# The last tokens' product with v, in three parts between the groups of h

## The chip, the cores and the metric

The kernel runs on one core of a Trainium2 chip. A core has five engines that run side by side, each with its own instruction stream: TensorE (PE, the matmuls; its weight loads are listed apart as PEld), VectorE (DVE), ScalarE (ACT), GpSimd (POOL) and SyncE (SP, which here issues nearly all transfers). Data lies in SBUF, results of matmuls in PSUM; a transfer (DMA) moves data between HBM and SBUF or within SBUF. The metric is the time of one execution on the device in microseconds (us); lower is better.

## The reference

Eight batches of eight heads, each with 576 tokens of 64 numbers, all in float32. Attention with a threshold: per row only the scores within tau of the row's maximum count. The result, 4,608 tokens of 512 numbers, goes through a feed-forward block.

```python
scores = scale * np.matmul(q, k.transpose(0, 1, 3, 2))
thresh = np.max(scores, axis=-1, keepdims=True) - tau
scores = np.where(scores >= thresh, scores, -1000000000.0)
attn = np.exp(scores - np.max(scores, axis=-1, keepdims=True))
attn = attn / (np.sum(attn, axis=-1, keepdims=True) + 1e-09)
x = np.matmul(attn, v)            # then (B,H,S,D) -> (B*S, H*D)
h = x @ w_in                      # 4608 x 512 @ 512 x 1024
solu = h * softmax(h)
ln = (solu - mean(solu)) / np.sqrt(var(solu) + 1e-06) * g_ln
out = ln @ w_out                  # 4608 x 1024 @ 1024 x 512
```

## The kernel before

**Tiles.** Two heads are always worked on at once. A batch's 576 tokens are 512 (two kinds, 0 and 1, of 256 tokens) and the last 64 (kind 2). The work of attention is a list of 144 slots, 18 for each batch: 8 for kind 0 and 8 for kind 1 (four pairs of heads, two slots each), and 2 for kind 2, in which two pairs of heads share a slot. A slot is 128 rows of scores for each of two heads.

**TensorE.** Nearly all matmuls are done on quarters of the array, 64 x 64, four side by side. A float32 matmul of the program appears in the trace as two weight loads and two matmuls, so four instructions; a group of four matmul records is one in each quarter.

**Rounds.** The main loop (lines 784 to 924) does one round for each slot and writes out the order of every engine by hand; nothing is reordered afterwards. In a round, TensorE gets first the transposes that fit beside the scores, then the scores of the slot (L412: 8 matmuls), then one step of the feed-forward block and, if one is due, one product with v. The steps of the feed-forward block for a tile of 128 tokens are: h in two halves of 512 columns (L572, `ff_h`, 16 matmuls each, in two successive rounds), and o in two halves (L676, `ff_o`, 32 matmuls each, later). The product with v (L516, `attend_steps`) multiplies v by the transposed attention `wT`; for kinds 0 and 1 it has 36 matmuls with 128 columns, and for kind 2 it has 72 with 64 columns, one such product for each batch. `attend_steps` is a generator: each step of it issues one matmul.

**The other engines in a round.** DVE takes the maxima of the scores (L434), ACT forms the ramp and the exponentials (L449, L458), POOL normalises (L468), DVE transposes (L480), and SP moves the result into `wT` in four transfers (L491); the product follows at least two rounds later. For h, DVE takes the maximum (L587), ACT the exponential (L596), DVE multiplies (L602), and so on until ACT or DVE writes the normalised tile V (L638, L643), which is transposed for o (L664). The output tile is copied out of PSUM by ACT (L691).

**PSUM.** Two tiles, s0 and s1, hold the scores. Two more, p0 and p1, are handed out in turn by `take` to h, to the products and to o. h keeps its tile until DVE has multiplied (L602); a product's is free after ACT has copied it into `xh` or `xe` (L539); that of o after ACT's copy into `ob` (L691). In a round that starts h and also has a product, h takes one tile and the product the other.

**Around the change.** When a product of kind 2 is due in a round that also has a half of h, the round passes the generator to `ff_h` as `beside`. The 16 matmuls of a half of h go in four groups of four (`c` from 0 to 3); after a group, `ff_h` may take a number of steps from the generator. Any rest is issued after `ff_h` by the round itself (lines 896 to 898). After the product comes ACT's copy into `xe` (`attended`, L539). In the first half of h a small instruction on POOL (`fence`, L107) waits for its last four matmuls, and the second half waits for that. For h tiles made after the last slot, `ff_h` uses the whole array (L562) and does nothing with `beside`.

Of the eight products of kind 2, seven are placed beside h: those of the batches 0, 2, 4 and 6 beside a second half, and those of 1, 3 and 5 beside a first half. The eighth comes after the last slot.

## Time and profile before

| what | value |
|---|---|
| median of five runs | 900.38 us (897.79 to 903.31) |
| the profiled execution | 897.58 us |
| its span, first to last instruction | 895.6 us |
| PE busy | 848.5 us, 95% |
| DVE busy | 680.6 us, 76% |
| ACT busy | 591.0 us, 66% |
| POOL busy | 452.7 us, 51% |
| L572, one matmul of h, 512 columns | 589 ns, 1856 records |
| L516, one matmul of a product, 64 or 128 columns | 264 ns on average, 5760 records |

The profile is of one execution, whose own time is the span and some 2 us around it. Matmuls overlap each other: a record's length says how long one took to pass through, not how far apart two can start. In a row of the timeline the first number is the start in us from the span's start, the second the length of the merged row, and the bracket at the end the idle time of the engine before it with what ended it. "issue" there means that the engine waited for nothing that the profile shows.

### The profile page before, as it was taken

How to read it: one execution, taken by the hardware profiler on the slowest of the kernel's cores; microseconds unless marked ns; L12 is line 12 of the kernel's file. 1: busy time of each engine (PE TensorE's matmuls, PEld its weight loads, DVE VectorE, ACT ScalarE, POOL GpSimd, SP SyncE). 2: the span in 40 equal slices, each digit the busy share in tenths (PEclk: the TensorE clock that was granted, in tenths of full speed). 3: DMA queues.
4: the chain of work that ended last, by engine and by line, in shares of the span. 5: the costliest groups of instructions: out<-in, count | busy, mean ns of one | idle time of the engine just before them, and what ended most of it. 6: DMA issues, size and time to landing. Idle time of an engine off the chain costs nothing. (4 is left out here: it accounts for less than half of the span.)

```text
span 895.6 us, 39683 instructions
## 1 busy us (share of the span) xinstructions
PE 848.5 (95%) x17089; PEld 646.1 (72%) x17089; DVE 680.6 (76%) x1312; ACT 591.0 (66%) x1241; POOL 452.7 (51%) x871
## 2 busy tenths in 40 slices
PE   5667899999999999999999999999999999999997
PEld 3445578877687777887787777878778787777655
DVE  5999786888777768777777777777877877887451
ACT  5866676777677767777677776677767776676121
POOL 2555555555555555555655555555555555555120
PEclk9688899999999999999999999999999999999999
DMA  7999989796867776876887777777877766766322
GB/s 241 257 240 243 216 191 206 180 214 159 202 158 176 164 177 158 189 175 159 188 187 179 164 160 185 182 175 157 190 184 176 179 134 146 167 139 134 78 48 48
DMA packets 95502, 154.61 MB, mean 173 GB/s; under 512 B 27224, under 2 KB 69216, under 8 KB 95328
## 3 DMA queue, kind: packets, MB, share of 16 engines
q1 hardware_dynamic: 94192, 150.09, 72.1%
q8 instruction: 134, 2.20, 1.1%
q10 hardware_dynamic: 1136, 2.00, 0.7%
q14 instruction: 40, 0.33, 0.1%
HBM read 46.14 MB, written 9.44 MB: 62 GB/s over the span
## 5 line engine op out<-in xcount | busy, mean ns | idle before, releaser
L434 DVE CUSTOM_DVE_ANT_0 w<-s_ps,tau_t 128x576 f32<-128x576 f32 x280 | 200.8, 754 | 135.0 <-PE s_ps L412 114.5
L449 ACT ACTIVATE w<-s_ps,nth 128x576 f32<-128x576 f32 x280 | 202.0, 744 | 120.0 <-DVE nth L434 97.4
L676 PE MATMUL o_ps<-w,uT 64*64 64x256 f32 x4608 | 269.3, 376 | 2.0 <-DVE uT L664 1.0
L676 PEld LDWEIGHTS o_ps<-w,uT 64*64 64x64 f32 x4608 | 232.1, 133 | 46.2 <-issue 11.9
L468 POOL TENSOR_SCALAR w<-w,sm 128x576 f32<-128x576 f32 x288 | 218.7, 772 | 14.3
L572 PE MATMUL h_ps<-w,xh 64*64 64x512 f32 x1856 | 220.9, 589 | 1.9 <-issue 1.9
L458 ACT ACTIVATE w<-w,ntau 128x576 f32<-128x576 f32 x288 | 220.4, 772 | 0.0
L480 DVE STREAM_TRANSPOSE T<-w 128x576 f32<-128x576 f32 x288 | 206.0, 751 | 5.6 <-POOL w L468 5.1
L516 PEld LDWEIGHTS pv<-wT,v 64*64 64x64 f32 x5760 | 170.1, 136 | 38.1 <-issue 23.1
L412 PE MATMUL s_ps<-kT,qT 64*64 64x64 f32 (+1 forms) x2048 | 175.4, 426 | 13.8 <-ACT w L449 12.8
L516 PE MATMUL pv<-wT,v 64*64 64x128 f32 (+1 forms) x5760 | 172.3, 264 | 7.4 <-DMA wT<-T 3.8
L572 PEld LDWEIGHTS h_ps<-w,xh 64*64 64x64 f32 x1856 | 114.1, 133 | 86.4 <-issue 62.7
L465 POOL TENSOR_SCALAR sm<-sm 128x2 f32<-128x2 f32 x144 | 37.5, 261 | 260.7 <-ACT w L458 257.8
L466 POOL TENSOR_TENSOR sm<-sm,mone 128x2 f32<-128x2 f32 x144 | 105.1, 730 | 12.0
L412 PEld LDWEIGHTS s_ps<-kT,qT 64*64 64x64 f32 x2048 | 68.6, 140 | 22.3 <-ACT w L449 18.1
L638 ACT ACTIVATE V<-u,nb,rs 128x1024 f32<-128x1024 f32 x36 | 44.7, 1241 | 52.7 <-POOL nb L628 52.7
L539 ACT COPY xh<-pv 128x256 f32<-128x256 f32 x64 | 23.7, 371 | 65.5 <-PE pv L516 65.5
L587 DVE TENSOR_REDUCE hm<-h_ps 128x1 f32<-128x1024 f32 x36 | 43.1, 1198 | 19.3 <-PE h_ps L572 13.1
L458 ACT ACTIVATION_READ_ACCUMULATOR w<-w,ntau 128x1 f32 x288 | 57.0, 198 | 0.0
L596 ACT ACTIVATE u<-h_ps,hm 128x1024 f32<-128x1024 f32 x36 | 40.3, 1119 | 19.2 <-DVE hm L587 13.9
L664 DVE STREAM_TRANSPOSE uT<-V 128x1024 f32<-128x1024 f32 x36 | 43.9, 1220 | 9.0 <-DMA V<-u 8.9
L602 DVE TENSOR_TENSOR u<-h_ps,u 128x1024 f32<-128x1024 f32 x36 | 42.8, 1189 | 10.0 <-ACT u L596 10.0
(81 smaller groups left out, 632.6 us busy)
## 6 DMA issues: line engine op xcount, KB each, us to landing
wT<-T SPq DMA_DIRECT2D x288, 288.0 KB, 5.8
V<-u SPq DMA_DIRECT2D x144, 64.0 KB, 3.7
out_dram<-ob SPq DMA_DIRECT2D x71, 128.0 KB, 3.0
v<-in_v_dram SPq DMA_DIRECT2D x16, 512.0 KB, 6.8
v<-in_v_dram SPq DMA_DIRECT2D x32, 256.0 KB, 5.7
q<-in_q_dram SPq DMA_DIRECT2D x15, 512.0 KB, 6.5
k<-in_k_dram SPq DMA_DIRECT2D x15, 512.0 KB, 6.4
raw<-in_moe_w_out_dram SPq DMA_DIRECT2D x8, 512.0 KB, 7.6
```

The costliest lines, as they stand in the source:

```text
L412: nc.tensor.matmul(out=ps[h][ROWS[y], ks], lhsT=lhsT, rhs=d["kT"][ROWS[h], ks], start=True, stop=True,)
L434: nc.vector.tensor_tensor_reduce(out=w, in0=ps[:, 0:S], in1=(zero if loose else tau_t).to_broadcast([P, S]), scale=1.0, scalar=BIG, op0=AL ...
L449: nc.scalar.activation(out=d["w"][x], in_=d["w"][x] if d["loose"] else d["ps"][x][:, 0:S], func=AF.Prelu, bias=d["nth"][x], scale=-1.0, al ...
L458: nc.scalar.activation(out=w, in_=w, func=AF.Exp, bias=ntau, scale=1.0, accum_out=sm[:, x : x + 1])
L466: nc.gpsimd.tensor_tensor(out=sm, in0=sm, in1=mone, op=ALU.pow)
L468: nc.gpsimd.tensor_scalar(out=w, in0=w, scalar1=sm[:, x : x + 1], scalar2=1.0, op0=ALU.mult, op1=ALU.mult)
L480: nc.vector.transpose(out=T[:, :, r, h, :], in_=w)
L516: nc.tensor.matmul(out=to, lhsT=d["v"][ROWS[u], h0 + h, m ^ 4 * u if m < 8 else m], rhs=rhs, start=m == 0, stop=m == NK - 1,)
L572: mm = nc.tensor.matmul(out=h[ROWS[y], f], lhsT=x[ROWS[r], c, ROWS[y]], rhs=w1_parts[ROWS[r], c, part ^ r], start=part == 0 and c == 0, st ...
L638: nc.scalar.activation(out=V, in_=u, func=AF.Identity, bias=nb, scale=rs)
L664: nc.vector.transpose(out=uT, in_=d["V"].rearrange("p y (m x) -> p m y x", x=32))
L676: nc.tensor.matmul(out=d["o"][ROWS[z], 512 * r : 512 * r + 256], lhsT=d["uT"][ROWS[r], m].rearrange("p y x -> p (y x)"), rhs=w2[ROWS[r], m ...
```

## The change

Before, the 72 matmuls of a product of kind 2 are issued after the third group of h (in the code also after the fourth, but then none are left). After, 24 are issued after the second, the third and the fourth group each.

```diff
                     if part and not last:
                         sync(mm, d["fence"])
                     last.append(mm)
-            for _, _ in zip(range(72 * (c > 1)), beside):
+            for _, _ in zip(range(24 * (c > 0)), beside):
                 pass
         if part == 0:
             d["fence"] = fence(last[-4:])
```

So TensorE's order, in matmuls of the program, goes at seven places from 12 of h, 72 of the product, 4 of h to 8 of h, 24 of the product, 4 of h, 24 of the product, 4 of h, 24 of the product. The order on DVE, ACT, POOL and SP stays, and so do all instructions and the waits that they carry.

## The prediction

> **What bounds the kernel now.** I read the page's head and busy rows first, then the clock row, then the list of waits, and then TensorE's own order of time around the seven places that the diff touches.

> ```profile
> span 895.6 us, 39683 instructions
> PE 848.5 (95%) x17089; PEld 646.1 (72%) x17089; DVE 680.6 (76%) x1312; ACT 591.0 (66%) x1241; POOL 452.7 (51%) x871
> PE   5667899999999999999999999999999999999997
> PEclk9688899999999999999999999999999999999999
> q8 instruction: 134, 2.20, 1.1%
> ```

> TensorE is busy in 95% of the span and in nine tenths or more of every slice from about 130 us on, at full clock. No other engine comes near. Busy is no proof of a bound, since a matmul's recorded length (589 ns for 512 columns) overlaps the next one; so I looked at the starts. Groups of four matmuls start 0.43 us apart in h with no hole, and between 100 and 880 us there are only eleven holes of more than 0.6 us between the starts of two TensorE records. So a microsecond more or less on TensorE's queue in this stretch is a microsecond in the span, and what happens on DVE, ACT or POOL counts only if TensorE then waits.

> Eight of those eleven holes have one thing in common. If all TensorE records (weight loads, matmuls, semaphore instructions) are numbered in order of start, each of the eight stands before a number that leaves 193 when divided by 256: at 104, 139, 226, 236, 332, 538, 648 and 743 us. The queue of kind "instruction" in the fence moves 2.20 MB in 134 packets, 16,384 bytes each: 256 instructions of 64 bytes. These are waits for the engine's own instructions, and three of the eight lie inside the product that the change moves. The third place, in TensorE's order of time:

> ```profile
> 330.28 1.90 PE L516 MATMUL pv<-wT,v 64*64 64x64 f32 x114
> 333.82 0.38 PE L516 MATMUL pv<-wT,v 64*64 64x64 f32 x9 [1.64 <-issue]
> 333.99 0.61 PE L572 MATMUL h_ps<-w,xh 64*64 64x512 f32 x3
> ...
> 334.10 1.02 PE L572 MATMUL h_ps<-w,xh 64*64 64x512 f32 x5
> 334.85 1.25 PE L412 MATMUL s_ps<-kT,qT 64*64 64x64 f32 x16
> ```

> The product has nine tenths of its matmuls done, then TensorE stands still for 1.64 us although it waits for no engine and no transfer ("issue"), and goes on. At 538 us the same hole is 0.43 us and at 743 us 0.70 us. In starts the three cost more: h and the product take 5.54 us where nothing stalls (below), here 7.45, 6.20 and 6.57 us from h's start to the next scores, so 1.91, 0.66 and 1.03 us. The instruction packet that ends the hole at 333.8 us ran from 331.19 to 332.25 us, 1.57 us before work resumed; at the other two the distance is 1.25 and 1.49 us.

> At the fourth and sixth place the product starts late for another reason, seen in the row of weight loads and in ACT's:

> ```profile
> 437.01 0.24 PEld L572 LDWEIGHTS h_ps<-w,xh 64*64 64x64 f32 x4 [0.19 <-issue]
> 437.83 1.30 PEld L516 LDWEIGHTS pv<-wT,v 64*64 64x64 f32 x78 [0.58 <-ACT ob L691]
> ```
> ```profile
> 436.07 1.24 ACT L638 ACTIVATE V<-u,nb,rs 128x1024 f32<-128x1024 f32 x1 [1.20 <-POOL nb L628]
> 437.21 0.57 ACT L691 COPY ob<-o_ps 128x512 f32<-128x512 f32 x1
> ```

> The product's PSUM pair is given back by the copy of an output tile on ACT, which ends at 437.78 us. Today that costs nothing: the last group of h before the product starts at 437.55 us and the product at 437.87 us, exactly in step. But there is no reserve.

> [...] the product's first weight loads run 0.32 us before its first matmul, under h. So a seam between h and the product need not cost anything.

> **The change part by part.** It removes and adds nothing: no instruction, no wait, no transfer; DVE, ACT, POOL and SP keep their order. Since the count is the same, the 256-instruction boundaries fall on the same numbers. Only TensorE's order changes, at seven places (the eighth batch's product goes beside h that isn't split, and stays).

> Prices, from the first place, where nothing stalls: the product's 72 matmuls (144 records) take from 134.38 to 136.48, 2.10 us, so 24 take 0.70 us; four matmuls of h (8 records, the starts 136.48 to 137.34) take 0.86 us. The order 12 h, 72, 4 h becomes 8 h, 24, 4 h, 24, 4 h, 24. Sum either way 16 x 0.215 + 2.10 = 5.54 us. Hence the product starts 0.86 us earlier and ends 0.86 us later, and h ends 0.70 us earlier.

> *Seams.* There are three more changes between the two kinds at each place. From h into the product the step is 0.32 to 0.43 us, h's own; from the product into h the first h matmul starts 0.01 us after the last of the product. I take zero; with a seam at 0.05 us (a few product matmuls' spacing of 15 ns) it would be 21 x 0.05 = 1.05 us lost, and a gain has no ground.

> *Instruction stalls in the product (third, fifth, seventh place).* Count instructions from h's start, four per matmul. One boundary is crossed at about number 55, the next at 311. Before, 55 lies 7 into the product and 311 lies 263 into it: both in the dense stretch, 256 x 7.3 ns = 1.9 us apart. After, 55 lies 23 into the first third and 311 lies 55 into the last: 1.72 + 0.17 = 1.89 us and 1.72 + 0.70 + 0.86 + 0.70 + 0.86 + 0.40 = 5.24 us from h's start, 3.35 us apart. At the third place h starts at 327.40 and instructions resume at 333.81, 6.4 us later. If the fetch lands when it does now, 1.2 us of stall stays, but only 41 instructions (0.30 us) stand behind it and no h: the window ends at 334.1 rather than 334.85, 0.74 us gained. If the fetch follows the crossing, which comes 0.74 us earlier, 1.4 us is gained. At 538 us instructions resume 5.16 us from h's start, before they are wanted: all 0.66 us gained. At 743 us they resume 5.54 us from it, 0.3 us late: 0.73 us gained, or all 1.03. Together 2.1 us, between 1.3 (fetches that come 0.4 us later each) and 3.1.

> *Stalls just after the window.* The hole at 139 us (0.97 us) belongs to the fetch of a boundary at number 152, in the product's first half before, in the second third after, crossed at the same time (3.34 us from h's start)[...] I take 0.4. The one at 648 us (a step of 0.91 us between starts where 0.32 is usual: 0.59 us) is absorbed by the delay of the sixth place, below.

> *Lost cover, fourth and sixth place.* The product now wants its pair at 437.01 and gets it at 437.83; the wait is no longer under h. 0.82 us each, 1.64 us, less the 0.59 us at 648: 1.05 us lost. Behind the waiting weight load stand the other eight matmuls of h and the next scores; those feed DVE, ACT and POOL, all with less load.

> *Lost cover, wT.* At the third and fifth place the last piece of wT is issued at 322.84 and 528.70 us and lands 6.3 us later, 329.1 and 535.0 us. The product's first matmul comes at 329.98 and 535.85 now, and would at 329.12 and 534.99: reserve 0.86 before, none after. In this profile it costs 0.0; a transfer that is later by some tenths costs them. I take 0.2 us for both, between 0 and 1.7.

> *The end of the product.* ACT's copy of xe starts 0.86 us later relative to the window. At the odd places the next o takes that pair: the copy (0.37 us) ends about 0.64 us after the product, o's weights then load in 0.13 us, and o's first matmul comes 0.97 us after the scores start. Hidden by the scores; 0. ACT is idle there (its idle before the copy is up to 2.5 us); if it ran an exponential of 0.77 us at that moment, up to 0.5 us would be lost.

> *h earlier.* The maximum on DVE starts 0.7 us earlier at the odd places, and the next scores' maximum some 0.3 us. TensorE's next scores start at 339.28, 0.4 us after their release by ACT at 338.88, so it doesn't wait for these now: 0 gained.

> Sum: -2.1 - 0.4 + 1.05 + 0.2 = -1.25 us, a span of 894.4; with the bounds above, -1.3 to -3.8 of gains and 1.05 to 3.8 of losses. The profiled execution took 897.6 us with a span of 895.6, 2.8 us below the median of 900.38. Taken off the median: 899.1 us.

> **Rivals.** (1) *The stalls were longer in the other runs.* The profiled run is the fast end; if the three in the product are each about 2 us elsewhere, 1.4 us is won at each, 4.2 + 0.4 - 1.25 = 3.35 us, 897.0. For it: instruction packets start anywhere from 2.2 us before to 4.2 us after the crossing of their boundary in this trace. Against: only three boundaries. (2) *Slower: the start of the product becomes a wait.* ACT's copy at 437.2 and 642 us, and wT at three places, come after TensorE wants them. From 0 reserve each further 0.1 us late costs 0.1; all 0.86 us at five places would be 4.3 us, against a gain of 2.5: 902.2. It decides as soon as the five waits average over 0.5 us. For it: two of them are at 0.82 in the trace. Against: the other three stand at 0 or have 0.3 us over (743 us). (3) *Nothing moves*: fetches and the copy shift along with TensorE; 900.4.

> **How the numbers follow.** Forecast 0.50, rival 1 0.17, rival 2 0.15, rival 3 0.18. The five runs spread by 5.5 us, so a median is good to about 1.2 us, and about 0.5% (4.5 us) is what can be told from no change. No case in its middle reaches that: 0.08 faster, from the tail of rival 1; 0.05 slower, from that of rival 2; 0.87 same. The range, from rival 1 with some scatter to most of rival 2, is 896.0 to 902.2.

> **What would show it.** Right: in TensorE's order of time the holes "issue" inside the product at about 333, 538 and 743 us are gone or below 1.2 us; at about 437 and 642 us the product's first weight load waits some 0.8 us for the copy of ob; the starts of h and of scores elsewhere keep their 0.43 us. Wrong: waits for wT of over 0.3 us at several places, or new holes at other 256-instruction boundaries, or a step of more than 0.5 us at a seam.

## The result and the profile after

| | before | after |
|---|---|---|
| median of the comparison | 898.42 us (893.13 to 904.42, 71 runs) | 896.87 us (892.65 to 900.46, 36 runs) |
| ratio | 1 | 0.9976, 95% interval 0.9965 to 0.9987 |
| span of the profiled execution | 895.6 us | 895.6 us |

By the ratio the change wins 0.24%, some 2.2 us; forecast were 1.25 us and "no change that counts". On two more occasions, told below, the ratio was 1.0004 and 0.9988, with intervals that include 1. So the gain is between nothing and a quarter of a per cent. Ratios leave out runs that lie more than 1.5% above the fastest of their kernel.

The page of the changed kernel, its head, busy row and TensorE's slices:

```profile
span 895.6 us, 39683 instructions
PE 849.3 (95%) x17089; PEld 663.1 (74%) x17089; DVE 681.0 (76%) x1312; ACT 591.4 (66%) x1241; POOL 452.5 (51%) x871
PE   5667899999999999999999999999999999999997
```

Nothing has moved at this height: the same bound, the same instructions, and by chance the same span. In the profile after, the first h that the change touches starts at 133.00 us rather than 131.81, so 1.2 us had been lost before the change could act. The difference has to be looked for at the seven places (numbered in order of time, one for each of the batches 0 to 6). At the third, TensorE's row of time now reads:

```profile
330.43 0.91 PE L516 MATMUL pv<-wT,v 64*64 64x64 f32 x43
...
331.30 1.03 PE L572 MATMUL h_ps<-w,xh 64*64 64x512 f32 x6
331.99 1.33 PE L516 MATMUL pv<-wT,v 64*64 64x64 f32 x47
333.11 0.23 PE L412 MATMUL s_ps<-kT,qT 64*64 64x64 f32 x3
```

The hole of 1.64 us is gone; the last third of the product takes 1.33 us, 0.42 us longer than the third before it (0.91 us). At the fifth place it went the other way:

```profile
536.98 0.67 PE L516 MATMUL pv<-wT,v 64*64 64x64 f32 x29
539.10 0.50 PE L516 MATMUL pv<-wT,v 64*64 64x64 f32 x18 [1.45 <-issue]
539.39 0.23 PE L412 MATMUL s_ps<-kT,qT 64*64 64x64 f32 x3
```

Here 1.45 us of "issue" where the kernel before had 0.43, at the same boundary of a 256-instruction block. And at the fourth place the lost cover, in the weight loads' row and in ACT's:

```profile
434.42 0.24 PEld L572 LDWEIGHTS h_ps<-w,xh 64*64 64x64 f32 x4 [0.19 <-issue]
436.09 0.83 PEld L516 LDWEIGHTS pv<-wT,v 64*64 64x64 f32 x46 [1.43 <-ACT ob L691]
```
```profile
434.33 1.24 ACT L638 ACTIVATE V<-u,nb,rs 128x1024 f32<-128x1024 f32 x1 [1.19 <-POOL nb L628]
435.47 0.57 ACT L691 COPY ob<-o_ps 128x512 f32<-128x512 f32 x1
```

ACT's copy ends at 436.04 us as late in the round as before, and the product that is now wanted 0.86 us sooner waits for it. In the list of waits the second of these rows is one that the kernel before doesn't have; the first was 2.8 us there, in three waits:

```profile
PE pv L516 <- issue: 2.5, 3, 1.4
PE pv L516 <- ACT ob L691: 1.0, 2, 0.5
```

Three profiles of the changed kernel and two of the one before were taken in all. The length of each place, from the first matmul of h to the first matmul of something else, in us (5.53 where nothing stalls):

| kernel | 1 | 2 | 3 | 4 | 5 | 6 | 7 | sum |
|---|---|---|---|---|---|---|---|---|
| before | 5.53 | 5.53 | 7.45 | 5.56 | 6.19 | 5.56 | 6.56 | 42.4 |
| before, again | 5.53 | 5.53 | 10.11 | 5.54 | 6.44 | 5.54 | 6.52 | 45.2 |
| after | 5.53 | 6.00 | 5.95 | 6.41 | 7.34 | 6.41 | 6.20 | 43.8 |
| after, again | 5.53 | 5.64 | 5.95 | 6.41 | 6.30 | 6.41 | 5.88 | 42.1 |
| after, third | 5.53 | 5.99 | 5.91 | 6.39 | 5.59 | 6.39 | 6.31 | 42.1 |

Places 2, 4 and 6 are longer by 0.1 to 0.9 us every time, 1.8 to 2.2 us together. Places 3, 5 and 7 are shorter on the whole and vary. What lies outside the places counts too. Summing all steps between TensorE's starts that stand at a block boundary (record number leaving 193 on division by 256), from 100 to 870 us, where the step is over 0.45 us, less 0.25 us each: 7.7 and 10.0 us before, 2.9, 5.3 and 4.2 us after. I call this the sum of block waits below.

That sum can be tested against the time. From the start of h at place 1 to the end of the span, the 14 profiles of this document took 758.5 to 771.2 us. Three things are taken off: the block waits of that stretch, the waits of the product's first weight load at places 2, 4 and 6 (counted in the same way), and half of any stretch at half clock (1.7 us each, in four profiles; see the last section). Twelve profiles are then left with 756.8 to 758.1 us. The other two, 759.7 and 759.9 us, are the two versions below that put idle matmuls in front of the kernel before; their 2 us are not explained. In the first pair of profiles the block waits of that stretch fall from 6.6 to 2.9 us, and the waits of the product's weights rise from nothing to 2.2 us.

### The profile page after: what moved, and what is told of

It reads as the page before. It is cut to its first block, busy times and chain, and to the rows that moved or that the text cites. A ratio compares the mean times of both kernels' runs of the same rounds, so it can differ in the third digit from the quotient of the medians.

```text
span 895.6 us, 39683 instructions
## 1 busy us (share of the span) xinstructions
PE 849.3 (95%) x17089; PEld 663.1 (74%) x17089; DVE 681.0 (76%) x1312; ACT 591.4 (66%) x1241; POOL 452.5 (51%) x871
## 2 busy tenths in 40 slices
PE   5667899999999999999999999999999999999997
## 5 line engine op out<-in xcount | busy, mean ns | idle before, releaser
L676 PEld LDWEIGHTS o_ps<-w,uT 64*64 64x64 f32 x4608 | 235.9, 133 | 41.8 <-ACT xh L539 10.1
L572 PE MATMUL h_ps<-w,xh 64*64 64x512 f32 x1856 | 223.7, 590 | 0.2 <-issue 0.2
L516 PEld LDWEIGHTS pv<-wT,v 64*64 64x64 f32 x5760 | 176.5, 136 | 43.9 <-issue 21.6
L412 PE MATMUL s_ps<-kT,qT 64*64 64x64 f32 (+1 forms) x2048 | 177.8, 426 | 13.9 <-ACT w L449 12.9
L516 PE MATMUL pv<-wT,v 64*64 64x128 f32 (+1 forms) x5760 | 177.1, 264 | 8.6 <-DMA wT<-T 4.1
L572 PEld LDWEIGHTS h_ps<-w,xh 64*64 64x64 f32 x1856 | 122.2, 134 | 72.4 <-issue 40.2
L412 PEld LDWEIGHTS s_ps<-kT,qT 64*64 64x64 f32 x2048 | 69.7, 141 | 20.3 <-ACT w L449 18.5
L638 ACT ACTIVATE V<-u,nb,rs 128x1024 f32<-128x1024 f32 x36 | 44.7, 1241 | 52.9 <-POOL nb L628 52.9
L602 DVE TENSOR_TENSOR u<-h_ps,u 128x1024 f32<-128x1024 f32 x36 | 42.8, 1189 | 10.8 <-ACT u L596 10.8
L664 DVE STREAM_TRANSPOSE uT<-V 128x1024 f32<-128x1024 f32 x36 | 43.8, 1218 | 6.8 <-DMA V<-u 6.8
```

What stands on the lines that cost most here:

```text
L412: nc.tensor.matmul(out=ps[h][ROWS[y], ks], lhsT=lhsT, rhs=d["kT"][ROWS[h], ks], start=True, stop=True,)
L516: nc.tensor.matmul(out=to, lhsT=d["v"][ROWS[u], h0 + h, m ^ 4 * u if m < 8 else m], rhs=rhs, start=m == 0, stop=m == NK - 1,)
L572: mm = nc.tensor.matmul(out=h[ROWS[y], f], lhsT=x[ROWS[r], c, ROWS[y]], rhs=w1_parts[ROWS[r], c, part ^ r], start=part == 0 and c == 0, st ...
L638: nc.scalar.activation(out=V, in_=u, func=AF.Identity, bias=nb, scale=rs)
L664: nc.vector.transpose(out=uT, in_=d["V"].rearrange("p y (m x) -> p m y x", x=32))
L676: nc.tensor.matmul(out=d["o"][ROWS[z], 512 * r : 512 * r + 256], lhsT=d["uT"][ROWS[r], m].rearrange("p y x -> p (y x)"), rhs=w2[ROWS[r], m ...
```

## The experiments

Two questions: is the hole "issue" a wait for the engine's instructions, and how do the gain and the lost cover split? Theory A is that of the prediction. B: the gain comes from the order on TensorE as such, or from h ending earlier. C: the holes belong to something else at those places.

### The two kinds of place apart

Three parts only where the product stands beside a second half of h (places 1, 3, 5, 7):

```diff
-            for _, _ in zip(range(72 * (c > 1)), beside):
+            for _, _ in zip(range(24 * (c > 0) if part else 72 * (c > 1)), beside):
```

> Three parts of 24 only where the product stands beside a second half of h (places 1, 3, 5, 7); beside a first half (2, 4, 6) the 72 stay behind the third group. Theory A (spreading the product shortens the waits for instruction blocks, and starting it earlier costs cover at places 4 and 6, and at 2 as the profile after shows): keeps the gain, loses none of the cover, so 1 to 2 us faster than the changed kernel, 3 to 4 us (0.35 to 0.45%) faster than the kernel before, and no weight load of the product waits for the copy of ob. Theory B (the gain comes alike from all seven places, from the order on TensorE alone): four sevenths of the changed kernel's 2.15 us, 1.2 us.

Measured: 895.23 us against 899.02 us, ratio 0.9961 (0.9941 to 0.9981). Places 2, 4 and 6 are back at 5.53 to 5.54 us, 3, 5 and 7 at 6.09, 5.53 and 6.28; the sum of block waits is 1.4 us. At the fourth place the weight load waits for the copy again only under h:

```profile
434.52 0.31 PEld L572 LDWEIGHTS h_ps<-w,xh 64*64 64x64 f32 x4
435.33 1.79 PEld L516 LDWEIGHTS pv<-wT,v 64*64 64x64 f32 x112 [0.49 <-ACT ob L691]
```

(The expectation that no such wait is left was wrong in words: it is there, as in the kernel before, and costs nothing.) The other half of the change alone:

```diff
-            for _, _ in zip(range(72 * (c > 1)), beside):
+            for _, _ in zip(range(72 * (c > 1) if part else 24 * (c > 0)), beside):
```

> The other part alone: three parts of 24 at places 2, 4 and 6 only. Theory A: slower than the kernel before by 0.5 to 1.7 us, with waits of 0.3 to 1.1 us for the copies of ob and xh before the product at these three places. Theory B: faster by three sevenths of 2.15 us, 0.9 us.

Measured: 899.13 us, ratio 1.0006 (0.9989 to 1.0023). No gain, as A says, though the loss isn't clear of zero. Its trace has places 2, 4 and 6 at 6.17, 6.40 and 6.39 us, 2.4 us over the stall-free length, and the sum of block waits at 5.2 us. The two halves multiply to 0.9967. B, a gain alike from all places, asks for 0.9987 in the first of these two kernels, outside its interval.

### Where the product starts, and how dense it is

```diff
-            for _, _ in zip(range(72 * (c > 1)), beside):
+            for _, _ in zip(range(36 * (c > 1)), beside):
```

> 36 matmuls behind the third and 36 behind the fourth group of h, at all seven places. The product starts where it does before, so no cover is lost; the boundaries at places 3, 5 and 7 lie some 2.8 us apart rather than 1.9 or 3.35. Theory A: faster than the kernel before by 1.5 to 2.5 us, as fast as the changed kernel or up to 1 us faster. Theory B (what counts is that h ends earlier, here 1.05 us rather than 0.70 us): 3 us faster.

Measured: 896.41 us, ratio 0.9964 (0.9950 to 0.9978), 2.6 us by the medians. The start is where it was (2.57 us from h's start), places 2, 4 and 6 have 5.53 to 5.56 us, so the cover is kept; places 3, 5 and 7 have 6.45, 5.53 and 5.92 us. The time doesn't tell the theories apart: B asked for 3 us, A for 1.5 to 2.5. The profiled execution was the longest of its 22, 899.8 us of span, with holes of 2.4 and 2.2 us in o that end at 143 and 250 us and a sum of block waits of 7.3 us, as much as the kernel before has; so it doesn't show where the gain of the median run comes from.

All of h first, and the product in one piece behind it:

```diff
-            for _, _ in zip(range(72 * (c > 1)), beside):
+            for _, _ in zip(range(0), beside):
```

> All 16 matmuls of h first, then the 72 of the product in one piece. h ends 2.1 us earlier than before, and the product starts 0.86 us later. Theory A (instruction blocks): the product is as dense as before, the boundaries at places 3, 5 and 7 lie 2.3 us apart rather than 1.9: 0 to 1 us faster than before. Theory B (h that ends earlier lets DVE and ACT go on earlier): more than the changed kernel's gain, over 3 us.

Measured: 905.44 us, ratio 1.0066 (1.0042 to 1.0091). Both theories missed it. B expected the most from this kernel, since h ends 2.1 us earlier in it, and it is slower than the kernel before. Waits for blocks don't hide a gain: with block waits and half clock taken off as above, 757.8 us are left, no less than elsewhere. That form of B is dead. A expected next to nothing. The seven places themselves are the best of all, 39.4 us, nearly without stalls; the holes stand behind them. TensorE in the round after the fourth place:

```profile
440.59 1.19 PE L412 MATMUL s_ps<-kT,qT 64*64 64x512 f32 x9
441.44 1.88 PE L572 MATMUL h_ps<-w,xh 64*64 64x512 f32 x12
445.52 1.01 PE L572 MATMUL h_ps<-w,xh 64*64 64x512 f32 x5 [2.19 <-issue]
```

The boundary inside the product (some 153 instructions from h's start) is crossed about a third into it, as before, and the next one comes 256 instructions on, in the following round. Before, the last group of h stood between the two, 16 instructions that take 0.86 us; now it is product, scores and the start of the next step alone. The block isn't there in time: the holes are 2.2 us after the fourth place, 2.3 after the sixth, 2.0 after the first. The sum of block waits is 10.8 us. This explanation came after the run; it fits A's mechanism. My step was too narrow: I had looked at the boundaries of places 3, 5 and 7 alone.

### Moving the boundaries, and nothing else

In front of the first transposes, where TensorE waits for k, the kernel before gets 32 matmuls of the identity: 128 instructions, whose results nobody reads.

```diff
+        for n in range(32):
+            nc.tensor.matmul(
+                out=tiles[n % 2][ROWS[n // 2 % 2], 960:1024],
+                lhsT=ident[ROWS[n // 2 % 2], ROWS[n // 2 % 2]],
+                rhs=ident[ROWS[n // 2 % 2], ROWS[n // 2 % 2]], start=True, stop=True,
+            )
         turned(first, [k_item(0), q_item(0, slice(0, 1)), e_item(0)])
```

> The kernel before with 32 added matmuls of the identity at the very start, where TensorE waits for k, so that 128 more instructions stand ahead of everything and each boundary of a 256-instruction block falls 128 instructions earlier in the work; nothing else is changed, and the product stays in one piece. Theory A (the holes are waits for instruction blocks): the holes inside the product at places 3, 5 and 7 go; boundaries now lie at the product's start and end at places 1, 4 and 6 (27 and 283 instructions from h's start) and 2 (87 and 343), so holes of 0.3 to 2 us appear there. Time: within 2 us of the kernel before. Theory C (the holes come from something at those places in the work, a transfer or the memory): they stay at 3, 5 and 7.

The third place in its trace, the product in one piece as before:

```profile
327.58 1.62 PE L572 MATMUL h_ps<-w,xh 64*64 64x512 f32 x12
328.87 2.27 PE L516 MATMUL pv<-wT,v 64*64 64x64 f32 x141
...
331.83 1.31 PE L412 MATMUL s_ps<-kT,qT 64*64 64x64 f32 x16
```

No hole. Places 3, 5 and 7 have 5.53 us each, 1 and 2 have 6.24 and 6.91 us. Places 4 and 6, where A expected holes too, have none (5.54). Of the eleven steps of more than 0.6 us between TensorE's starts from 100 to 870 us, nine again stand at numbers that leave 193 on division by 256, now 128 instructions earlier in the work; the sum of block waits is 8.0 us. C is out; the holes go with the count of instructions. The instruction packets agree: in the profile before there are 134 for 34,178 matmuls and weight loads of TensorE, one for 255, and if they are matched to the blocks in order, then in all 14 profiles, from 100 to 880 us, no boundary is crossed sooner than 1.2 us after the end of the packet that brings the block behind it.

What the shift does to the time stays open. The ratio is 1.0027 (0.9997 to 1.0057), but it rests on half of the 20 runs, which spread from 897.20 to 922.46 us (the kernel before: 893.36 to 906.21). The profiled execution, 899.16 us, is the fourth shortest; what the long ones do was not seen.

A shift that should help, 45 matmuls, 180 instructions:

> The kernel before with 45 matmuls of the identity at the start, 180 instructions; the product stays in one piece. From the starts in the traces, with the holes taken out and 4 us (2.9 to 5.1) from the crossing of one boundary to the block behind the next, the waits for blocks between 100 and 870 us sum to 7.9 us as it stands, 4.3 us with a shift of 180 (the least of all) and 11.3 us with 128. Theory A: 2 to 4.5 us faster than the kernel before, as much as the changed kernel or more, without moving the product. Theory C (the holes have nothing to do with blocks): 0 to 1 us slower, by the added matmuls.

Measured: 898.35 us, ratio 1.0005 (0.9976 to 1.0033). A miss. Places 3, 5 and 7 are clean (5.53 us each), which is 3.6 us of the profile before, but new holes stand elsewhere, one of them right behind the third place:

```profile
332.72 1.25 PE L412 MATMUL s_ps<-kT,qT 64*64 64x64 f32 x16
333.69 0.59 PE L676 MATMUL o_ps<-w,uT 64*64 64x256 f32 x3
336.41 2.08 PE L676 MATMUL o_ps<-w,uT 64*64 64x256 f32 x24 [2.12 <-issue]
```

The sum of block waits is 9.8 us where I had reckoned 4.3. One latency of about 4 us for every block is too simple: in the profile before, the packet for the next block starts anywhere from 2.2 us before a boundary is crossed to 4.2 us after. What decides it was not settled. The profiled execution here, 905.05 us, was also the longest of its 14.

### The same kernels again

> The kernel before once more, for a second profile: ratio 1.000 within its interval. Theory A: the holes are at the same boundaries, those at places 3, 5 and 7 among them, but of other sizes, 0.3 to 2.5 us each.

Measured: ratio 0.9994 (0.9966 to 1.0022). The holes stand at the same boundaries at places 3, 5 and 7, with 4.6, 0.9 and 1.0 us over the stall-free length where the first profile had 1.9, 0.7 and 1.0. The large one, beyond the 2.5 us expected, is shown at the end; this execution, 903.95 us, was the longest of its 12.

> The changed kernel once more, for a second profile: ratio 0.9976 within its interval. Theory A: holes in the last third of the product at places 3, 5 and 7 between 0 and 1.5 us each, less in sum than in the kernel before; the waits before the product at places 2, 4 and 6 are there again, 0.3 to 0.5 us at 2 and 0.8 us at 4 and 6.

Measured: 1.0004 (0.9985 to 1.0023); the expected 0.9976 lies outside. The waits before the product at places 4 and 6 are there again, 0.82 us each; at place 2 only 0.1 us were lost.

> The changed kernel a third time, on the same chip as the three beside it. Theory A: between the two ratios seen, 0.9976 and 1.0004: 0.9985, and 1.5 to 2.5 us above the version with three parts beside second halves alone.

> Three parts of 24 beside second halves alone, again, beside the changed kernel on the same chip. Theory A: 0.9965 of the kernel before, 1.5 to 2.5 us below the changed kernel (the 0.3 to 0.85 us of cover that places 2, 4 and 6 lose). If the two lie within 0.5 us of each other, the lost cover is made up elsewhere.

Side by side on one chip: the changed kernel 898.01 us, ratio 0.9988 (0.9962 to 1.0013); the version with second halves alone 895.06 us, 0.9972 (0.9953 to 0.9992). It lies 2.9 us below by the medians, in the direction that the lost cover asks for and a little more than expected. The intervals of the two ratios overlap, but the runs of the two versions compared directly (14 and 22, resampled) give an interval of 1.3 to 4.4 us for the difference of the medians.

### Versions that keep both

```diff
-            for _, _ in zip(range(72 * (c > 1)), beside):
+            for _, _ in zip(range(24 * (c > 0) if part else 36 * (c > 1)), beside):
```

> Three parts of 24 beside second halves of h, and two parts of 36 behind the third and fourth group beside first halves, where the product must not start earlier. Theory A: no lost cover and no more dense stretch: as fast as the version with three parts at second halves alone or up to 1 us faster, 3.5 to 4.5 us below the kernel before (0.9950 to 0.9961).

Measured: 895.69 us against 898.32, ratio 0.9969 (0.9950 to 0.9987); places 2, 4 and 6 at 5.53 to 5.59 us, block waits 1.4 us. That is short of what was expected, and no better than second halves alone. With the shift of 180 instructions on top:

> Three parts beside second halves, two parts of 36 beside first halves, and the same shift of 180 instructions. By the same sum the waits for blocks go from 5.5 us (this version without the shift) to 3.0 us. Theory A: 4.5 to 6 us faster than the kernel before (0.9933 to 0.9950), the fastest here.

Measured: 895.22 us against 898.28, ratio 0.9964 (0.9942 to 0.9986), short of what was expected; the shift gives nothing that can be told. Three parts at second halves alone (0.9961 and 0.9972) remain the simplest version that is faster than the kernel before each time.

## Why the prediction was right, and where it wasn't

**The bound, and the size.** Right: 899.1 us was forecast from 900.38, a gain of 1.25 us; the ratios say 2.2, -0.4 and 1.1 us. A few tenths of a per cent, and no side of 0.5% was reached. The measured 896.87 us lies 2.2 us below the 899.1, but 2.0 us of that is the base: the kernel before has a median of 898.42 us in the comparison, not the 900.38 of its first five runs.

That the sum came out so close is in part luck. In the first pair of profiles block waits fell by 3.7 us, for which the forecast has 2.1 + 0.4 + 0.59 = 3.1, and the waits before the product came to 2.2 us, for which it has 1.64 + 0.2. But only 0.7 us was gained inside the product at places 3, 5 and 7, for which the forecast has 2.1; the rest fell away at boundaries elsewhere, and of these the forecast had counted two. Of the rivals, only the first of the three ratios rules out number 3 (nothing moves). The long stalls of number 1 came at one of three places in the second profile of the kernel before (4.6 us over), and the waits of number 2 came to 2.2 us, under the 2.5 from which it would have decided.

**Seams.** Right: at the first place the length is 5.53 us in every profile but two, in whatever pieces the product comes; those two (5.93 us with two parts, 6.24 with the shift of 128) have a block boundary inside. Three more changes between h and product cost 0.00 us. One reading was off: at the first place the first weight loads run 0.42 us ahead of the first matmul, not 0.32.

**Stalls in the product.** The mechanism was right: the shift of 128 shows that the holes belong to block boundaries. The size (2.1 us gained, between 1.3 and 3.1) was a sum over one profile's latencies, and these scatter: places 3, 5 and 7 together had 3.6 and 6.5 us over the stall-free length before, and 2.9, 1.5 and 1.2 us after. In the pair of profiles that belongs to the result the gain is 0.7 us, against the first profile after with its late block at 538 us. The hole there, 1.45 us, also breaks the sign that was named, gone or below 1.2 us; in the other two profiles all three places keep to it. And the lower end was added up wrongly: with every fetch 0.4 us later the three places gain some 0.3 us each, 1.0 rather than 1.3.

**Stalls just after the window.** Undersized. The hole at 139 us, for which I took 0.4 us as an estimate, is gone in all three profiles after (1.35 us from start to start before, 1.69 when taken again). In the first of them the packet with the block for this boundary starts 4.7 us after the start of h at the first place, in the profile before 5.7 us, and the boundary is crossed at 7.2 us in both: the block came 1.0 us sooner for the same crossing. But one at 153 us, 0.95 to 1.23 us, was there in all three, where the kernel before had none in one profile and 0.83 us in the other. The prediction had named new holes at other boundaries as a sign of being wrong, and against the first profile this is one. The hole at 648 us, "absorbed", is gone in all three, but it wasn't in the second profile of the kernel before either.

**Lost cover, places 4 and 6.** Right: 0.82 us each forecast; in each of the three profiles the two places take 6.39 to 6.41 us rather than 5.56, so 0.83 to 0.85 us.

**Lost cover, place 2.** Missed; no step of the prediction names it. What gives the pair back there is ACT's copy of xh. In the trace of before it ends 1.0 us after h's start (228.03 us); the product, 0.86 us sooner, would start 1.72 us after it: a reserve of 0.7 us. In the profile after, where h starts at 227.78 us, the copy ends 2.1 us after h's start, and the product waits. Its rows before and after, and the weights after:

```profile
228.69 0.35 ACT L539 COPY xh<-pv 128x256 f32<-128x256 f32 x1
```
```profile
229.50 0.36 ACT L539 COPY xh<-pv 128x256 f32<-128x256 f32 x1
```
```profile
229.91 0.83 PEld L516 LDWEIGHTS pv<-wT,v 64*64 64x64 f32 x46 [1.02 <-ACT xh L539]
```

The reserve had come from a hole: before, TensorE waited for a block 1 us ahead of h (the hole that the prediction lists at 226 us, 0.97 us from start to start), while ACT went on. In the profile after this hole is gone, and a part of what that gained is lost again to the copy. The other profiles agree: in all nine without a hole there the copy ends 2.0 to 2.1 us after h's start, whatever the kernel, and in the second profile after, where the hole is 2.05 us from start to start, it ends before h starts. The place cost 0.47, 0.11 and 0.46 us in the three profiles.

**wT.** The reserve that was none at places 3 and 5 held: the product starts 1.72 us from h's start in all three profiles, 0.2 us forecast, 0.0 measured. Rival 2, in which these waits decide, needed them.

**h earlier.** Right that it gains nothing: the kernel in which h ends earliest is 0.66% slower than the one before, and no faster with its waits for blocks taken off.

## What to carry to other kernels

Where TensorE runs streams of small matmuls, number its records in order of start and see whether the unexplained holes share a remainder modulo 256. Here they did (193), and no boundary was crossed sooner than 1.2 us after the end of the packet with the block behind it. Long matmuls mixed between the short ones took the sum of block waits from 7.7 to 2.9 us in the first pair of profiles, and to 1.4 us with three parts at second halves alone. Mix them without moving the start of a stream ahead of what it waits for: here an earlier start cost some 2 us at three places, more than half of what the mixing gained. Take more than one profile of each version, too: the sizes of these holes differ from one execution to the next (at the third place of the kernel before, 1.64 and 3.35 us). And a hole that vanishes from a window has perhaps only gone to the next boundary, so look one block further on before counting a gain (with the shift of 180 the third place was clean, and 2.12 us stood right behind it).

## What was not expected of the hardware

A wait for instructions can cost more than itself. In the second profile of the kernel before, the third place has a hole of 3.35 us, and then the granted clock falls. First the row of TensorE, then three windows, whose columns are length, busy time of PE, PEld, DVE, ACT and POOL with instructions, TensorE's granted clock, DMA share and GB/s:

```profile
339.49 0.58 PE L516 MATMUL pv<-wT,v 64*64 64x64 f32 x9 [3.35 <-issue]
```
```profile
331.00:336.00 5.00, 5.00 (x166) 3.95 (x158) 4.31 (x8) 3.35 (x7) 1.52 (x3) 1.00 0.74 168
336.00:339.60 3.60, 0.25 (x13) 0.11 (x9) 0.00 (x0) 0.00 (x0) 2.27 (x4) 0.98 1.09 271
339.60:342.50 2.90, 2.90 (x30) 1.68 (x34) 0.57 (x1) 0.37 (x1) 0.00 (x0) 0.50 0.95 240
```

For 3.41 us, from 339.47 us on, TensorE has half its clock, and the place is 4.58 us over its stall-free length instead of some 3.3. Half clock for 3.41 us also followed shorter holes: of 2.42 us (the version with two parts), 2.01 us (all of h first) and 2.12 us (the shift of 180), while holes of 2.17 us in the first of these and of 2.19 and 2.27 us in the second left the clock whole.
